# Filling only the empty rows of a row buffer with one scatter, and three loads and feature steps in another order

## The chip, the cores and the metric

The kernel runs on one core of a Trainium2 chip. The metric is the device time of one execution in microseconds (us), smaller is better. Three runs of the kernel before gave 189.14, 189.53 and 187.53 us, a median of 189.14. A core has five engines with a queue each: PE (matrix multiply, with its weight loads), DVE (vector), ACT (scalar), POOL (GpSimd) and SP (here it only issues transfers). Each engine works its own instructions in the order in which they were written; a semaphore makes one wait for another or for a transfer.

## The reference

```python
# q, k, v: (4, 4, 1088, 32) float32; S1, S2: (8, 32)
def phi(x):
    a = einsum('rd,bhsd->bhsr', S1, x); b = einsum('rd,bhsd->bhsr', S2, x)
    return einsum('bhsi,bhsj->bhsij', a, b).reshape(*x.shape[:-1], 64)
q_p, k_p = phi(q), phi(k)
kv = einsum('bhsf,bhsd->bhfd', k_p, v); z = sum(k_p, axis=2)
x  = einsum('bhsf,bhfd->bhsd', q_p, kv) / (einsum('bhsf,bhf->bhs', q_p, z)[..., None] + 1e-6)
x  = x.transpose(0, 2, 1, 3).reshape(4352, 128)          # rows: batch by position
expert = token_ids * 2654435761 % 8                      # 4352 ids
for e in range(8):                                       # w1[e]: 128x1024, w2[e]: 1024x128
    out[expert == e] = maximum(x[expert == e] @ w1[e], 0) @ w2[e]
```

## The kernel before

**Attention.** The four batches are worked one after the other in the order 0, 2, 1, 3 (counted b = 0 to 3 below). Each has 1024 "main" positions, held as 8 blocks of 128, and a "tail" of 64; the tails of two batches share one tile (`k_tail`, `v_tail`, `q_tail`). For a main tile of k or q, PE turns it (`kT_ps`, L460), ACT copies the turned blocks (`kT`, L465), PE multiplies by S1 and S2 (`abk_ps`, `abq_ps`, L486), ACT copies the first half (`first_of_ab`, L511) and DVE makes the 64 features (`kp` of k, `f` of q, L524, two instructions of 128x1024). PE then sums `kv` over positions (L557), turns the features of q (`fT_ps`, L575) and multiplies by `m`, the diagonal of `kv` (`x_ps`, L586). DVE normalizes in three chunks of three instructions (`den`, `den`, `xs`, L602 to L604). The tail of q goes the same way: `qTt_ps` (L471), `abqt_ps` (L501), `f_tail`, `fTt_ps` (L812). For b = 2 and 3, DVE's own 32x32 transposes turn q instead (`qT`, L494).

**Routing.** Every row goes to a slot of its expert. The ids (`tok`, `tok_tail`) give a mask, a scan and counts (`cnt`, L384), from which `place` (the expert's rank), `left` and the row number `sidx` come. An expert has 256 early slots and `cap` late ones, 313 for the first in rank and 5 fewer for each one behind it: 2048 + 2364 = 4412 slots for 4352 rows. Rows that fit no slot would be worked by a loop at the end (`turns`, L1128).

**The row buffer.** `x_rows` in device memory has a region of 256 + 4352 rows for each expert. Before any row is written, `fill_rows` fills the first 256 + 320 rows of each region with zeros and an id that no output row has (L207, four transfers), and 128 rows behind the regions (L210). POOL then scatters each normalized block of 128 rows into it by `sidx` (L609, 34 times), and SP fetches the rows expert by expert (`fetch`, L770).

**Experts.** Sixteen groups g (early and late slots of eight experts) are worked: PE `hp` (L912) and `op` (L920), ACT and DVE evict, rows come and go through SP and POOL. Between them DVE works `overflow_tables` in eight places.

**Order.** All five queues are written by hand. `pace` (L141) lets a large load start only when the third before it has landed. The loads stand on SP's queue in the order of the code; `tail(0)` of the ids and `tok` stand on ACT's queue, `tail(1)` on POOL's.

Of the kernel before, what the change touches and what calls it, by code (L numbers as in the profile page):

```python
# [30 lines left out]
def kernel(  # L31
# [35 lines left out]
    FL = -(-2 * GL // P) * P // 2  # L67
# [5 lines left out]
    OT = -(-(N - caps[-1]) // P)  # L73
# [51 lines left out]
    def load_tok():  # L125
# [69 lines left out]
    q_t.append(load_main(q, 1, "q"))  # L195
# [3 lines left out]

    def fill_rows():  # L200

        regions = x_dram[1:1 + E * XR].rearrange("(e m) d -> e m d", m=XR)
        h = P // 2
        for lo, hi, p in ((0, GE, P), (GE, GE + FL, h)):
            n = (hi - lo) // p
            for es in (slice(0, E // 2), slice(E // 2, E)):
                pace(nc.sync.dma_start(regions[es, lo:hi].rearrange("e (p n) d -> p e (n d)", n=n),  # L207
                                       empty_row[0:p, 0:n].rearrange("p n d -> p (n d)").unsqueeze(1)
                                       .to_broadcast([p, E // 2, n * XW])))
        nc.sync.dma_start(x_dram[1 + E * XR:], empty_row[:, 0])  # L210

# [180 lines left out]
    def route_places(cnt):  # L392
# [12 lines left out]
                                       op0=OP.mult, op1=OP.add)  # L405

# [425 lines left out]
    qTt = tail_turned(q_tail, "qTt_ps")  # L832
# [10 lines left out]
    for b in range(1, B):  # L843
# [156 lines left out]
    past = const.tile([P, OT, E], F32)  # L1000
    te = const.tile([P, OT], F32)
    begin = const.tile([P, OT], F32)

    def overflow_tables():
        nc.vector.scalar_tensor_tensor(nt[:], place[:], float(GD), left[:], op0=OP.mult, op1=OP.add)
        nc.vector.tensor_scalar(nt[:], nt[:], float(P - 1 - GL), 0.0, op0=OP.add, op1=OP.max)
# [19 lines left out]
        nc.vector.tensor_scalar(begin[:], begin[:], float(P), None, op0=OP.mult)
# [46 lines left out]
    for i in range(8):  # L1073
# [55 lines left out]
    with tc.If(turns > 0):  # L1129
        with tc.For_i(0, turns):  # L1130

            of = moe.tile([P, 2], F32, tag="of", name="of", bufs=1)
# [4 lines left out]
            nc.vector.tensor_scalar(turn[:], turn[:], 1.0, None, op0=OP.add)
            hot = moe.tile([P, E], F32, tag="hot", name="hot", bufs=1)
            picked = moe.tile([P, 2, E], F32, tag="picked", name="picked", bufs=1)
            own = moe.tile([P, 2], F32, tag="own", name="own", bufs=1)  # L1140
            V = nc.vector
            V.tensor_scalar(hot[:], iota[:, 0:E], of[:, 0:1], None, op0=OP.is_equal)
            for i, t in enumerate((place, left)):
                V.tensor_tensor(picked[:, i], hot[:], t[:], op=OP.mult)
# [78 lines left out]
```

## Time and profile before

| | us |
|---|---|
| runs | 187.53, 189.14, 189.53 (median 189.14) |
| profiled execution, its own time | 189.09 |
| its span | 187.4 |
| PE busy | 171.6 (92%) |
| DVE busy | 95.9 (51%) |
| POOL busy | 78.5 (42%) |
| ACT busy | 63.0 (34%) |
| moved by transfers | 28.54 MB |

The times that runs give are of whole executions; the span is from the first to the last thing that the profile sees in one of them, 1.7 us less. A stretch is given as start:end in us from the span's start. "PEclk" is the clock that PE was granted, as a share of full speed. A timeline row has its start, its length from the first to the last of its instructions, the engine, line, operation, what is written from what, and how many; in brackets how long the engine had been idle before it, and what ended that.

### The profile page before, as it was taken

The page shows a single profiled execution, that of the slowest core. Times are in us where ns is not written, and L with a number is a line of the kernel's source. Part 1 is how long each engine was busy: PE and PEld are TensorE (multiplying, and loading weights), DVE is VectorE, ACT ScalarE, POOL GpSimd, SP SyncE. Part 2 cuts the span into 40 slices and gives each one's busy share as a digit, 9 for nine tenths or more (in the row PEclk, how much of TensorE's full clock was granted, in tenths as well). Part 3 has the DMA queues.
Part 4 walks back from the last instruction along what each step waited for, and adds up shares of the span by engine and source line. Part 5 has one row for each costly group of instructions (what it writes and reads, how often), then busy time and mean ns, then how long its engine had stood idle before and what let it go on. Part 6 is the DMA issues. An engine that isn't in the chain of part 4 may idle for free. (4 is left out here: it accounts for less than half of the span.)

```text
span 187.4 us, 4151 instructions
## 1 busy us (share of the span) xinstructions
PE 171.6 (92%) x1526; PEld 142.2 (76%) x1526; DVE 95.9 (51%) x289; ACT 63.0 (34%) x160; POOL 78.5 (42%) x125
## 2 busy tenths in 40 slices
PE   7789809997979999999999999999999999999990
PEld 2569708997868888788888887777777777777990
DVE  3387634569895825346525535445254754524330
ACT  2277423552714323233233223232331313311320
POOL 7375047507787787144134122142240403335762
PEclk9999975999999999999999999999999999999998
DMA  3999999998517988966675694441323232130110
GB/s 97 307 265 282 204 271 344 354 323 263 161 61 166 306 174 196 215 174 169 108 189 143 116 173 91 96 99 38 88 58 89 70 84 69 28 84 29 45 36 28
DMA packets 45204, 28.54 MB, mean 152 GB/s; under 512 B 22065, under 2 KB 42546, under 8 KB 45183
## 3 DMA queue, kind: packets, MB, share of 16 engines
q1 hardware_dynamic: 41983, 23.57, 49.4%
q0 software_dynamic: 2240, 4.53, 8.5%
q8 instruction: 12, 0.20, 0.5%
q10 hardware_dynamic: 960, 0.17, 0.5%
q14 instruction: 9, 0.07, 0.1%
HBM read 17.42 MB, written 7.09 MB: 131 GB/s over the span
## 5 line engine op out<-in xcount | busy, mean ns | idle before, releaser
L920 PE MATMUL op<-hT,w 128*128 128x256 f32 (+8 forms) x256 | 76.4, 389 | 0.0
L923 POOL DMA_INDIRECT out_dram<-os,put x35 | 34.2, 977 | 74.6 <-DVE put L779 44.2
L709 DVE TENSOR_SCALAR hT<-hp 128x256 f32<-128x256 f32 (+9 forms) x68 | 29.1, 429 | 55.5 <-PE hp L912 46.3
L920 PEld LDWEIGHTS op<-hT,w 128*128 128x128 f32 x256 | 47.5, 190 | 10.5
L707 ACT ACTIVATE hT<-hp 128x256 f32<-128x256 f32 (+9 forms) x68 | 26.4, 390 | 65.0 <-PE hp L912 63.5
L912 PE MATMUL hp<-xT_late,w 128*128 128x313 f32 (+8 forms) x144 | 42.0, 386 | 0.2 <-DVE xT_late L805 0.2
L609 POOL DMA_INDIRECT x_rows<-xs,sidx x32 | 31.4, 982 | 24.4 <-DVE xs L604 8.6
L912 PE MATMUL hp<-xT,w 128*128 128x256 f32 x128 | 37.0, 380 | 0.3 <-issue 0.2
L912 PEld LDWEIGHTS hp<-xT_late,w 128*128 128x128 f32 x144 | 25.4, 190 | 7.2 <-issue 0.6
L912 PEld LDWEIGHTS hp<-xT,w 128*128 128x128 f32 x128 | 24.0, 190 | 4.0 <-issue 0.5
L524 DVE TENSOR_TENSOR f<-first_of_ab,abq_ps 128x1024 f32<-128x1024 f32 x8 | 9.4, 1214 | 5.8 <-ACT first_of_ab L511 5.8
L524 DVE TENSOR_TENSOR kp<-first_of_ab,abk_ps 128x1024 f32<-128x1024 f32 x7 | 8.3, 1217 | 5.6 <-ACT first_of_ab L511 5.4
L798 DVE COPY xh<-xg 128x256 uint16<-128x256 uint16 (+1 forms) x28 | 9.8, 391 | 0.0
L575 PE MATMUL fT_ps<-ident,f 128*128 128x128 f32 x64 | 8.2, 278 | 1.6 <-DVE f L524 1.6
L557 PE MATMUL kv<-va,kp 128*64 128x66 f32 x256 | 8.5, 222 | 1.0 <-issue 1.0
L576 ACT COPY fT<-fT_ps 128x512 f32<-128x512 f32 x16 | 8.3, 598 | 2.6 <-PE fT_ps L575 2.4
L557 PEld LDWEIGHTS kv<-va,kp 128*64 128x64 f32 x256 | 8.0, 138 | 1.3 <-issue 1.3
L575 PEld LDWEIGHTS fT_ps<-ident,f 128*128 128x128 f32 x64 | 6.9, 141 | 2.3 <-DVE f L524 2.0
L465 ACT COPY kT<-kT_ps 128x512 f32<-128x512 f32 x12 | 6.6, 588 | 5.4 <-PE kT_ps L460 5.4
L586 PE MATMUL x_ps<-m,fT 128*64 128x66 f32 x256 | 8.3, 223 | 0.0
L586 PEld LDWEIGHTS x_ps<-m,fT 128*64 128x64 f32 x256 | 7.8, 137 | 0.2 <-issue 0.2
L981 DVE COPY os<-turned 128x256 uint16<-128x256 uint16 (+1 forms) x26 | 7.2, 315 | 0.9 <-DMA turned<-half 0.7
(158 smaller groups left out, 137.1 us busy)
## 6 DMA issues: line engine op xcount, KB each, us to landing
w<-in_moe_w_dram SPq DMA_DIRECT2D x16, 512.0 KB
q<-in_q_dram SPq DMA_DIRECT2D x4, 512.0 KB
v<-in_v_dram SPq DMA_DIRECT2D x4, 512.0 KB
xg<-x_rows SPq DMA_DIRECT2D x12, 129.0 KB
k<-in_k_dram SPq DMA_DIRECT2D x3, 512.0 KB
x_rows<-empty_row SPq DMA_DIRECT2D x2, 660.0 KB
x_rows<-empty_row SPq DMA_DIRECT2D x2, 528.0 KB
out_dram<-os,put POOLq DMA_INDIRECT x35, 2.7
```

What stands on the lines that cost most here:

```text
L524: eng.tensor_tensor(dst, a[:, r].unsqueeze(3).to_broadcast(shape), ab[:, r].unsqueeze(2).to_broadcast(shape), op=OP.mult)
L557: nc.tensor.matmul(kv[HALVES[x], z], f[:, x], w.rearrange("p h d -> p (h d)"), start=(n == 0 and z == 0), stop=(n == T), skip_group_check= ...
L575: nc.tensor.transpose(p[:, j, z], f[:, (t0 + j) // Q, z, (t0 + j) % Q].rearrange("p h f -> p (h f)"), ident[:])
L576: nc.scalar.copy(fT[:, t0:t0 + 2], p[:])
L586: nc.tensor.matmul(p[x, j, z], fT[:, t0 + j, z, x], m[:, z], start=True, stop=True, skip_group_check=True)
L609: st_ = G_.indirect_dma_start(out=x_dram[:], out_offset=bass.IndirectOffsetOnAxis(ap=sidx[:, c:c + 1], axis=0), in_=row, in_offset=None, b ...
L707: nc.scalar.activation(dst, src, AF.Relu if relu else AF.Copy)
L709: return nc.vector.tensor_scalar(dst, src, 0.0, None, op0=OP.max).ins
L798: nc.vector.tensor_copy(xh[:, x * w:(x + 1) * w].rearrange("p (a b) -> p a b", a=n), xg3[k][:, 0:n].bitcast(U16).rearrange("p a (b two) -> ...
L912: last_mm[0] = nc.tensor.matmul(hp[:, 0:hi - lo], w1[:, g % E, c * P:(c + 1) * P], x_columns(first_of(g) + lo, first_of(g) + hi), start=Tr ...
L920: nc.tensor.matmul(ops[g][:, 0:hi - lo], w2[:, g % E, c], hTs[g][:, c, lo:hi], start=(c == 0), stop=(c == FC - 1))
L923: st_ = nc.gpsimd.indirect_dma_start(out=out[:], out_offset=bass.IndirectOffsetOnAxis(ap=idx, axis=0), in_=src, in_offset=None, bounds_che ...
```

## The change

The four fills of `x_rows` go. In their place DVE works out, while the counts are at hand, which rows of the slots are empty (`route_free`, seven instructions, and `route_free_end`, eight), and POOL scatters one block of 128 empty rows to them (`empty_rows`); indices without a row lie out of bounds and are dropped. With more than 128 empty slots the late rows would all go to the loop at the end, whose tables and body are written anew for that (`few`). `q`'s second main load stands behind the tails of k and v, and `q_tail` behind the third loads of k and q. Both tails of the ids are loaded by POOL. The steps of q's tail move into the loop of b = 1, and for the last q the features stand ahead of the normalization of b = 2.

On SP's queue, from the load of v of b = 0 (`v0`) to the tail of q; digits behind a name count batches, the last number is only a buffer's. Before:

```order
L159 DMA v0_107<-in_v_dram 128x4x256
L159 DMA q1_109<-in_q_dram 128x4x256
L151 DMA k_tail_111<-in_k_dram 64x8x32 x2
L151 DMA v_tail_114<-in_v_dram 64x8x32 x2
L207 DMA x_rows<-empty_row_154 128x4x264 x2
L207 DMA x_rows<-empty_row_154 64x4x660 x2
L210 DMA x_rows<-empty_row_154 128x132
L159 DMA v1_162<-in_v_dram 128x4x256
L151 DMA q_tail_164<-in_q_dram 64x8x32 x2
L159 DMA k2_167<-in_k_dram 128x4x256
L159 DMA q2_169<-in_q_dram 128x4x256
```

And of the change, the same stretch of SP's queue:

```order
L155 DMA v0_106<-in_v_dram 128x4x256
L147 DMA k_tail_108<-in_k_dram 64x8x32 x2
L147 DMA v_tail_111<-in_v_dram 64x8x32 x2
L155 DMA q1_155<-in_q_dram 128x4x256
L155 DMA v1_157<-in_v_dram 128x4x256
L246 DMA x_rows<-empty_row_152 128x132
L155 DMA k2_160<-in_k_dram 128x4x256
L155 DMA q2_162<-in_q_dram 128x4x256
L147 DMA q_tail_164<-in_q_dram 64x8x32 x2
```

The four fills between the tails and `v1` are gone, `q1` stands behind the tails, and `q_tail` behind `q2`.

On PE's queue, from the turning of the second q to the sums of b = 1. Before:

```order
L460 MATMUL kT_ps_522<-ident_117,q1_109 128x128 x4
L471 MATMUL qTt_ps_569<-ident_117,q_tail_164 128x128 x2
L486 MATMUL abq_ps_574<-s_k_215,kT_520 64x4x16 x8
L486 MATMUL abq_ps_574<-s_k_215,kT_527 64x4x16 x8
L460 MATMUL kT_ps_593<-ident_117,k2_167 128x128 x4
L460 MATMUL kT_ps_600<-ident_117,k2_167 128x128 x4
L501 MATMUL abqt_ps_607<-s_k_215,kT_tail_572 64x64 x4
L557 MATMUL kv_620<-va1_145,kp_530 64x66 x32
```

And of the change:

```order
L484 MATMUL kT_ps_543<-ident_114,q1_155 128x128 x4
L510 MATMUL abq_ps_590<-s_k_211,kT_541 64x4x16 x8
L510 MATMUL abq_ps_590<-s_k_211,kT_548 64x4x16 x8
L484 MATMUL kT_ps_609<-ident_114,k2_160 128x128 x4
L484 MATMUL kT_ps_616<-ident_114,k2_160 128x128 x4
L581 MATMUL kv_628<-va1_143,kp_551 64x66 x32
L581 MATMUL kv_628<-va_tail1_141,kp_tail_230 64x66 x4
L495 MATMUL qTt_ps_670<-ident_114,q_tail_164 128x128 x2
L599 MATMUL fT_ps_676<-ident_114,f_623 128x128 x4
```

The turning of q's tail (`qTt_ps`) moved from ahead of `abq_ps` to behind the sums of b = 1; its products follow the four `fT_ps`.

On DVE's queue, at b = 2: the features of the last k (`kp`), the normalization of b = 2 (`den`, `xs2`) and the features of the last q (`f`). Before:

```order
L524 TENSOR_TENSOR kp_991<-first_of_ab_953,abk_ps_932 128x1024 x2
L602 TENSOR_SCALAR den_1013<-x_ps_956 128x12
L603 RECIPROCAL den_1013<-den_1013 128x12
L604 TENSOR_TENSOR xs2_191<-x_ps_956,den_1013 128x3x128
L602 TENSOR_SCALAR den_1026<-x_ps_969 128x12
L603 RECIPROCAL den_1026<-den_1026 128x12
L604 TENSOR_TENSOR xs2_191<-x_ps_969,den_1026 128x3x128
L602 TENSOR_SCALAR den_1039<-x_ps_982 128x8
L603 RECIPROCAL den_1039<-den_1039 128x8
L604 TENSOR_TENSOR xs2_191<-x_ps_982,den_1039 128x2x128
L524 TENSOR_TENSOR f_1049<-first_of_ab_1011,abq_ps_994 128x1024 x2
```

And of the change:

```order
L548 TENSOR_TENSOR kp_1012<-first_of_ab_974,abk_ps_953 128x1024 x2
L548 TENSOR_TENSOR f_1034<-first_of_ab_1032,abq_ps_1015 128x1024 x2
L626 TENSOR_SCALAR den_1037<-x_ps_977 128x12
L627 RECIPROCAL den_1037<-den_1037 128x12
L628 TENSOR_TENSOR xs2_187<-x_ps_977,den_1037 128x3x128
```

The two feature instructions `f` moved ahead of the nine of the normalization. The diff, without the loop at the end:

```diff
         def tail(x, eng):
             eng.dma_start(tok_tail[half_rows(x)], ids[2 * x:2 * x + 2, SM:].rearrange("u s two -> s u two"))
-        tail(0, nc.scalar)
         nc.scalar.dma_start(tok[:].rearrange("p (b t) two -> p b (t two)", b=B),
                             ids[:, 0:SM].rearrange("b (p t) two -> p b (t two)", t=T))
-        return lambda: tail(1, nc.gpsimd)
+        return lambda: [tail(x, nc.gpsimd) for x in range(TT)]
...
-    q_t.append(load_main(q, 1, "q"))
     k_tail = load_tail(k, "k_tail")
     v_tail = load_tail(v, "v_tail")
-    def fill_rows():
-        regions = x_dram[1:1 + E * XR].rearrange("(e m) d -> e m d", m=XR)
...
-    empty_row = const.tile([P, 2 * FL // P, XW], F32)
+    empty_row = const.tile([P, XW], F32)
...
-    fill_rows()
+    q_t.append(load_main(q, 1, "q"))
     v_t.append(load_main(v, 1, "v"))
-    q_tail = load_tail(q, "q_tail")
+    nc.sync.dma_start(x_dram[1 + E * XR:], empty_row[:])
     k_t.append(load_main(k, 2, "k"))
     q_t.append(load_main(q, 2, "q"))
+    q_tail = load_tail(q, "q_tail")
...
+    def route_free(cnt):
+        V = nc.vector
+        V.tensor_tensor(free[:, 0], took[:], cnt[:, 1, 0], op=OP.subtract)
+        V.scalar_tensor_tensor(free[:, 1], place[:], -float(GD), left[:], op0=OP.mult, op1=OP.subtract)
+        V.tensor_scalar(free[:, 1], free[:, 1], float(GL), 0.0, op0=OP.add, op1=OP.max)
+        V.tensor_tensor_scan(free_to[:].rearrange("p k e -> p (k e)"), ones[:, 0:NC * E],
+                             free[:].rearrange("p k e -> p (k e)"), 0.0, op0=OP.mult, op1=OP.add)
+        V.tensor_copy(row_at[:, 0], cnt[:, 1, 0])
+        V.tensor_scalar(row_at[:, 1], left[:], float(GE), None, op0=OP.add)
+        V.scalar_tensor_tensor(row_at[:], place[:].unsqueeze(1).to_broadcast([P, NC, E]), float(XR), row_at[:],
+                               op0=OP.mult, op1=OP.add)
+    def route_free_end():
...
+        V.tensor_scalar(eidx[:], row[:], float(FAR), None, op0=OP.add)
+    def empty_rows():
+        st_ = G_.indirect_dma_start(
+            out=x_dram[:], out_offset=bass.IndirectOffsetOnAxis(ap=eidx[:], axis=0),
+            in_=empty_row[:], in_offset=None, bounds_check=E * XR, oob_is_err=False)
...
     abt = tail_products(kTt, "abt_ps")
+    route_free(cnt)
     tail_features(kp_tail, first_copied(abt))
     route_early()
+    route_free_end()
+    empty_rows()
...
-    qTt = tail_turned(q_tail, "qTt_ps")
     abq = side_ab(qT, "abq_ps")
     firsts = first_copied(flat(abq))
     kT = side_turned(k_t[2])
-    abt = tail_products(qTt, "abqt_ps")
     f = all_features(firsts, "f", 1)
-    tail_features(f_tail, first_copied(abt))
...
         if b == 1:
             qT = q_blocks(q_t[2])
+            qTt = tail_turned(q_tail, "qTt_ps")
...
         fT = f_all(f)
         if b == 1:
-            tail_f_turned(f_tail)
+            tail_features(f_tail, first_copied(tail_products(qTt, "abqt_ps")))
...
         x_ps = x_all(b)
+        if b == 1:
+            tail_f_turned(f_tail)
...
+        if b == 2:
+            f = all_features(firsts, "f", 1)
         x_normalized(b, x_ps)
         if b == 1:
             x_tail(0, fT_tail)
             scatter_tail(0)
-        if more:
             f = all_features(firsts, "f", 1)
-        if b == 1:
             qT = q_blocks(q_t[3])
...
-    for i in range(8):
+    for i in range(5):
         at(G - 5 + i // 4, 2 * (i % 4), next, tables, None)
...
     with tc.If(turns > 0):
+        nc.gpsimd.drain()
         with tc.For_i(0, turns):
```

More of the change, by code (lines that the diff above doesn't have):

```diff
@@ L72 @@
     GAP = (ST - HT) * P - sum(caps)
-    OT = -(-(N - caps[-1]) // P)
+    OT = -(-(E * GE + N) // P) + E
     WARM = 9
@@ L405, in route_places @@
                                        op0=OP.mult, op1=OP.add)
+    free = const.tile([P, NC, E], F32)
+    free_to = const.tile([P, NC, E], F32)
+    row_at = const.tile([P, NC, E], F32)
+    nth = const.tile([P, NC, E], F32)
+    eidx = const.tile([P, 1], I32)
+    def route_free(cnt):
[10 more added lines that the diff above has]
+    def route_free_end():
+        V = nc.vector
+        within = const.tile([P, NC, E], F32, name="within")
+        V.tensor_tensor(nth[:], free[:], free_to[:], op=OP.subtract)
+        V.tensor_scalar(nth[:], nth[:], p1[:], None, op0=OP.add)
+        V.tensor_tensor(within[:], nth[:], free[:], op=OP.is_le)
+        V.scalar_tensor_tensor(within[:], nth[:], 0.0, within[:], op0=OP.is_gt, op1=OP.mult)
+        V.tensor_tensor(row_at[:], row_at[:], nth[:], op=OP.add)
+        V.scalar_tensor_tensor(row_at[:], row_at[:], -float(FAR), within[:], op0=OP.add, op1=OP.mult)
+        row = const.tile([P, 1], F32, name="row_of_free")
+        V.tensor_reduce(row[:], row_at[:].rearrange("p k e -> p (k e)"), axis=AX.X, op=OP.add)
+        V.tensor_scalar(eidx[:], row[:], float(FAR), None, op0=OP.add)
[3 more added lines that the diff above has]
+            in_=empty_row[:], in_offset=None, bounds_check=E * XR, oob_is_err=False)
+        tc.declare_no_dep(st_.ins, group="x_rows", reason="distinct rows")
+        tc.add_to_no_dep_group("x_rows", st_.ins)
     def route_rows(u, dst):
@@ L999 @@
     n_over = const.tile([P, 1], I32)
-    past = const.tile([P, OT, E], F32)
-    te = const.tile([P, OT], F32)
-    begin = const.tile([P, OT], F32)
+    begin = const.tile([P, E], F32)
+    few = const.tile([P, 1], F32)
     def overflow_tables():
-        nc.vector.scalar_tensor_tensor(nt[:], place[:], float(GD), left[:], op0=OP.mult, op1=OP.add)
-        nc.vector.tensor_scalar(nt[:], nt[:], float(P - 1 - GL), 0.0, op0=OP.add, op1=OP.max)
+        nc.vector.tensor_scalar(few[:], free_to[:, 1, E - 1:E], float(P), None, op0=OP.is_le)
+        nc.vector.tensor_scalar(begin[:], place[:], -float(GD), float(GL + GE), op0=OP.mult, op1=OP.add)
+        yield
+        nc.vector.tensor_tensor(begin[:], begin[:], few[:].to_broadcast([P, E]), op=OP.mult)
+        nc.vector.tensor_tensor(nt[:], left[:], begin[:], op=OP.subtract)
+        yield
+        nc.vector.tensor_scalar(nt[:], nt[:], float(GE + P - 1), 0.0, op0=OP.add, op1=OP.max)
         nc.vector.tensor_copy(nt_i[:], nt[:])
@@ L1138 @@
-            hot = moe.tile([P, E], F32, tag="hot", name="hot", bufs=1)
[L1139 to L1144, printed above, removed]
+            V = nc.vector
+            late_of = moe.tile([P, E], F32, tag="late_of", name="late_of", bufs=1)
@@ new lines @@
+            of = moe.tile([P, 1], F32, tag="of", name="of", bufs=1)
+            hot = moe.tile([P, E], F32, tag="hot", name="hot", bufs=1)
+            picked = moe.tile([P, 5, E], F32, tag="picked", name="picked", bufs=1)
+            own = moe.tile([P, 5], F32, tag="own", name="own", bufs=1)
+            V.tensor_tensor(late_of[:], ends[:], turn[:].to_broadcast([P, E]), op=OP.is_le)
+            V.tensor_reduce(of[:], late_of[:], axis=AX.X, op=OP.add)
+            V.tensor_scalar(hot[:], iota[:, 0:E], of[:], None, op0=OP.is_equal)
@@ L1145 @@
+            V.tensor_tensor(picked[:, 0], ends[:], nt[:], op=OP.subtract)
+            V.tensor_tensor(picked[:, 0], picked[:, 0], hot[:], op=OP.mult)
+            for i, t in enumerate((begin[:], place[:], left[:], cnt[:, 1, 0])):
+                V.tensor_tensor(picked[:, 1 + i], hot[:], t, op=OP.mult)
             V.tensor_reduce(own[:], picked[:], axis=AX.X, op=OP.add)
-            at = moe.tile([P, 4], F32, tag="at", name="at", bufs=1)
+            at = moe.tile([P, 6], F32, tag="at", name="at", bufs=1)
@@ new lines @@
+            V.tensor_scalar(at[:, 2:3], at[:, 0:1], float(GE), None, op0=OP.is_gt)
+            V.tensor_tensor(at[:, 1:2], at[:, 1:2], at[:, 2:3], op=OP.max)
+            V.tensor_scalar(at[:, 3:4], own[:, 3:4], float(GE), None, op0=OP.add)
+            V.tensor_tensor(at[:, 3:4], at[:, 0:1], at[:, 3:4], op=OP.is_le)
+            V.tensor_tensor(at[:, 1:2], at[:, 1:2], at[:, 3:4], op=OP.mult)
+            V.scalar_tensor_tensor(at[:, 4:5], own[:, 2:3], float(XR), at[:, 0:1], op0=OP.mult, op1=OP.add)
```

55 lines of the change are left out of this document (14 added, 41 removed).

## The prediction

> **What bounds the kernel now.** I read the page first, for the engine that is busiest:
>
> ```profile
> PE 171.6 (92%) x1526; PEld 142.2 (76%) x1526; DVE 95.9 (51%) x289; ACT 63.0 (34%) x160; POOL 78.5 (42%) x125
> ```
>
> PE leaves 187.4 - 171.6 = 15.8 us of the span. The second view was busy time by stretch (columns: length, then busy us of PE, PEld, DVE, ACT and POOL with instruction counts, granted clock, share of the transfer engines, GB/s):
>
> ```profile
> 21.50:27.85 6.35, 1.07 (x11) 0.86 (x9) 3.43 (x9) 1.88 (x3) 1.85 (x2) 0.85 0.97 242
> 27.85:32.73 4.88, 4.88 (x51) 4.10 (x52) 1.86 (x2) 1.95 (x5) 3.66 (x5) 0.50 1.05 345
> 38.93:57.50 18.57, 15.74 (x394) 14.44 (x390) 17.41 (x38) 7.29 (x16) 11.66 (x12) 1.00 0.59 184
> 61.55:183.00 121.45, 121.06 (x553) 99.51 (x553) 56.64 (x195) 34.87 (x99) 44.16 (x46) 1.00 0.49 113
> ```
>
> The experts (61.55 on) are PE without a gap, so what is gained there has to be gained by starting them earlier. The hole is 21.50 to 27.85, with the transfer engines full, and behind it PE works 4.88 us at half its clock. From 38.93 to 57.50 DVE is the full engine (17.41 of 18.57) and PE has slack. The third view, PE's waits (total, times, longest), names what ends the holes:
>
> ```profile
> PE qTt_ps L471 <- DMA q_tail<-in_q_dram: 5.3, 1, 5.3
> PE fT_ps L575 <- DVE f L524: 1.6, 1, 1.6
> PE cnt L384 <- ACT cp L379: 1.3, 1, 1.3
> PE kv L557 <- issue: 1.0, 1, 1.0
> ```
>
> All four lie in the attention, and the change touches the first three. The 1.0 us of "issue" waits for nothing that the profile shows.
>
> **Part 1: the fills and q's tail.** PE's timeline around the hole; the first two rows are the same work at full clock elsewhere:
>
> ```profile
> 12.69 1.09 PE L460 MATMUL kT_ps<-ident,k 128*128 128x128 f32 x8
> 40.14 1.10 PE L486 MATMUL abq_ps<-s_k,qT 128*64 128x64 f32 x32
> 21.48 1.09 PE L460 MATMUL kT_ps<-ident,q 128*128 128x128 f32 x8
> 27.85 0.66 PE L471 MATMUL qTt_ps<-ident,q_tail 128*128 128x128 f32 x2 [5.28 <-DMA q_tail<-in_q_dram]
> 28.44 1.98 PE L486 MATMUL abq_ps<-s_k,kT 128*64 128x64 f32 x32
> 30.34 1.97 PE L460 MATMUL kT_ps<-ident,k 128*128 128x128 f32 x8
> 32.24 0.67 PE L501 MATMUL abqt_ps<-s_k,kT_tail 128*64 128x64 f32 x8
> 32.73 2.06 PE L557 MATMUL kv<-va,kp 128*64 128x66 f32 x64
> ```
>
> `qTt_ps` waits for its load, and all of PE's queue stands behind it. Its load was late because of what stands ahead of it on SP's queue (the page's sizes, then SP's timeline):
>
> ```profile
> x_rows<-empty_row SPq DMA_DIRECT2D x2, 660.0 KB
> x_rows<-empty_row SPq DMA_DIRECT2D x2, 528.0 KB
> ```
>
> ```profile
> 8.57 0.37 SPq L159 DMA_DIRECT2D q<-in_q_dram  x1
> 11.87 6.29 SPq L207 DMA_DIRECT2D x_rows<-empty_row  x4
> ```
>
> The fills are 2 x 660 + 2 x 528 = 2376 KB, and `v1` stands behind them too. In the change the fills are gone. What is late next? ACT's and DVE's rows say it:
>
> ```profile
> 22.17 1.07 ACT L465 COPY kT<-kT_ps 128x512 f32<-128x512 f32 x2 [2.08 <-PE kT_ps L460]
> 27.04 1.05 ACT L541 COPY va<-v 128x1024 f32<-128x1024 f32 x1 [3.80 <-DMA v<-in_v_dram]
> ```
>
> ```profile
> 16.70 0.69 DVE L524 TENSOR_TENSOR kp_tail<-first_of_ab,abt_ps 128x512 f32<-128x512 f32 x1 [0.83 <-ACT first_of_ab L511]
> 20.12 1.22 DVE L524 TENSOR_TENSOR kp<-first_of_ab,abk_ps 128x1024 f32<-128x1024 f32 x1 [1.75 <-ACT first_of_ab L511]
> 23.12 1.21 DVE L524 TENSOR_TENSOR kp<-first_of_ab,abk_ps 128x1024 f32<-128x1024 f32 x1
> 38.93 2.35 DVE L524 TENSOR_TENSOR kp<-first_of_ab,abk_ps 128x1024 f32<-128x1024 f32 x2 [3.66 <-ACT first_of_ab L511]
> ```
>
> `va` of b = 1 needs `v1`, which landed at 27.04. Even at 345 GB/s, the best stretch above, the fills took 2376 x 1.024 / 345 = 7.1 us of the transfer engines, so `v1` lands by 20.0, ahead of 23.24, where ACT is done with `kT` and turns to it. `k2` (512 KB) stands right behind, 2.2 us more at 242 GB/s, so about 22.2, wanted at 23.8. `q1` now stands behind four tail loads, but it had waited for `q0` until 8.57 anyway, and it is wanted only at 21.48.
>
> So, from 21.48: both `kT` copied at 23.24, the second half of `abq_ps` behind it to 23.8, `k2` turned (1.09) to 24.9. `kv` there needs `va` (23.24 + 1.05 = 24.3) and the second `kp` (24.33, and later by part 2). I take 24.9 against 32.73: 7.8 earlier. Of this the wait is 5.28; the half clock is (1.98 - 1.10) + (1.97 - 1.09) and half of 0.66 + 0.67, 2.4; the two tail steps left this place (0.7 at full clock), and a wait for ACT's copies of about 0.6 shows that the hole had covered.
>
> The two tail steps come back behind `kv` (half of 0.66 and 0.67), while the turning of `f_tail` leaves the way to DVE's `kp` at 38.93 (row below, 0.60). `kv` to `kp` was 38.93 - 32.73 = 6.2, and becomes 6.2 + 0.7 - 0.6 = 6.3: `kp` at 31.2 instead of 38.93, 7.7 earlier. From there on DVE is the full engine, so this is what carries on.
>
> ```profile
> 36.75 0.60 PE L812 MATMUL fTt_ps<-ident,f_tail 128*128 128x128 f32 x4
> ```
>
> That turning (0.60) now stands between `kp` and PE's next `kv`, in the stretch that DVE fills: PE's slack there is 18.57 - 15.74 = 2.8, of which 1.6 lies at `fT_ps`, 1.0 is the "issue" hole, and 0.2 is left. If the hole stays, 0.6 - 0.2 = 0.4 reaches DVE; if it goes, nothing. I take 0.4 off.
>
> *On the clock.* The granted clock was 0.50 all the way from 27.85 to 32.73, though PE was busy throughout, so the recovery took above 4 us and is priced above at 2.4. The Trainium skill ("TensorE: Matmul & The Clock Gate", Part 1) says that an idle window of about 3.4 us halves PE's clock and a busy one of about 3.4 us restores it, so by it the pause would cost 3.4 x 0.5 = 1.7, and the sum would gain 0.7 less. The trace shows the halving; its recovery is longer here, and the row decides.
>
> **Part 2: what DVE and POOL get.** Fifteen small DVE instructions of 128x8 or 128x16. The nearest rows are six of `route_places`, from here to the `f` behind them:
>
> ```profile
> 12.38 0.17 DVE L394 SCALAR_TENSOR_TENSOR left<-took,counts 128x8 f32<-128x8 f32 x1
> 13.53 2.34 DVE L524 TENSOR_TENSOR f<-first_of_ab,abq_ps 128x1024 f32<-128x1024 f32 x2
> ```
>
> (13.53 - 12.38) / 6 = 0.19 each; my bounds are 0.17, the row's own length, and 0.28, half as much again. Seven are 1.3 us where DVE idled 0.83: `kp_tail` ends 0.5 later, at 17.9. Eight more are 1.5, with 0.5 carried over, where DVE idled 1.75: `kp` at 20.12 comes 0.3 later, the second at 24.6 instead of 24.33, still ahead of PE's 24.9. So 0; at 0.28 the fifteen take 1.3 more, 24.6 becomes 25.9, and 1.0 is lost. A gain is excluded, since nothing leaves DVE there.
>
> POOL gets one scatter more, and its scatters of rows no longer wait for the fills (the page's group: busy, mean ns, then idle time ahead and its longest releaser):
>
> ```profile
> L609 POOL DMA_INDIRECT x_rows<-xs,sidx x32 | 31.4, 982 | 24.4 <-DVE xs L604 8.6
> ```
>
> The 8.6 stands ahead of the first scatter; the `xs` it names follows the `kp` of 20.12 by a microsecond or so, so it was the fills that ended late. Without it the eight scatters of b = 0 start at about 22.5 and stand at most (31.4 + 24.4 - 8.6) / 32 = 1.5 apart, so they are through by 34.5. The first rows of b = 1 come about 0.9 behind `kp` at 31.2 + 2.35, at 34.5 too. The empty rows' scatter (0.98) stands ahead, at about 20.6, before any row is there: 0. The smaller fill of `empty_row` and eight overflow steps that become five run in DVE and POOL time that nobody waits for: 0.
>
> **Part 3: the ids.** `tail(0)` leaves ACT's queue, so `tok` is issued earlier; POOL works a second such load.
>
> ```profile
> 1.90 0.74 ACTq L130 DMA_DIRECT2D tok_tail<-in_moe_token_ids_dram  x1
> 7.75 0.18 DVE L367 TENSOR_SCALAR eid_i<-tok 128x32 int32<-128x32 int32 x1 [2.20 <-DMA tok<-in_moe_token_ids_dram]
> 10.37 1.95 POOL L524 TENSOR_TENSOR kp<-both_of_ab 128x1024 f32<-128x1024 f32 x1 [3.80 <-ACT counts L387]
> ```
>
> DVE waits 2.20 for `tok`, and PE's `cnt` stands 1.3 behind that chain. ACT issues `tok` 0.74 earlier, but it then shares the transfer engines with the first k. I take 0.6, between 0 (k delayed as much) and 1.3 (all of `cnt`'s wait). POOL's second load, about as long as ACT's, is covered by its 3.80 of idle time.
>
> **Part 4: features ahead of the normalization.** At b = 2:
>
> ```profile
> 50.24 2.35 DVE L524 TENSOR_TENSOR kp<-first_of_ab,abk_ps 128x1024 f32<-128x1024 f32 x2
> 52.81 0.37 ACT L511 COPY first_of_ab<-abq_ps 128x256 f32<-128x256 f32 x1 [2.23 <-issue]
> 55.14 2.34 DVE L524 TENSOR_TENSOR f<-first_of_ab,abq_ps 128x1024 f32<-128x1024 f32 x2
> 59.54 0.17 DVE L602 TENSOR_SCALAR den<-x_ps 128x12 f32<-128x12 f32 x1 [2.05 <-PE x_ps L586]
> 60.67 0.41 PE L789 MATMUL xp<-ident,xg 128*128 128x128 f32 x2
> ```
>
> On before's time axis: `f` can start when ACT has copied, 53.2, not 55.14, and PE's wait of 1.58 goes. The normalization (55.14 - 52.59 = 2.55) then runs 55.5 to 58.1, and the next one behind it without the 2.05 of idle time. The first transposed rows `xp` need the memory bank of its first chunk, at 58.1 + about 1.0 = 59.1 instead of 60.67. That caps the gain at 1.4; I take 1.3 (0.5 if the fetched rows come in late, which were not waited for at 60.67).
>
> **The sum.** 7.7 - 0.4 + 0 + 0.6 + 1.3 = 9.2 us, all ahead of the experts, whose 121 us of PE only move; 0.1 goes to a second branch on every engine at the end. 189.09 - 9.1 = 180.0 us. The profiled execution stands at the median of the runs (189.14), so I forecast 180.0 for the median too. The unknowns put together, 0.6 + 1.0 + 0.8 against the forecast and 0.7 + 0.4 for it, give 178.9 to 182.4 for this case.
>
> **The rivals.**
>
> *Another load takes over.* `v1` or `k2` is late. For: the transfer engines were full (0.97 to 1.05) up to here. Against: 7.1 us of their work went. If `v1` came only at 27.04 as before, `kv` starts at 28.1: 3.2 lost, 183.2, and up to 2.2 more if the clock falls again, 185.4.
>
> *DVE becomes the bound.* The fifteen instructions at 0.28, 1.0, and 0.3 more where the stretch from 38.93 is DVE's already: 181.3.
>
> *Part 4 gives nothing*, because the fetch of the first rows (on POOL's scatters of b = 1) decides: 181.3.
>
> *Slower: the scatter of empty rows stalls POOL.* 4412 - 4352 = 60 slots are empty if every row finds a slot, so 68 of 128 indices are dropped. If a dropped index were dear, POOL's chain slips, and with it the fetch of the first rows and the experts. The scatter starts 1.9 us ahead of the first rows (20.6 to 22.5), so it would have to take 1.9 + 9.1 = 11 us for the whole gain to go, 10 / 68 = 0.15 per dropped row; at twice that the time is 190 + 10 = 200. Against it:
>
> ```profile
> L923 POOL DMA_INDIRECT out_dram<-os,put x35 | 34.2, 977 | 74.6 <-DVE put L779 44.2
> ```
>
> These 35 scatters drop the same empty rows, and their mean is 0.977, against 0.982 for the rows that are all written.
>
> *The loop at the end is entered.* It is if a row finds no slot or more than 128 are empty. Before's execution ends without it, so every row has a slot and 60 are empty. I give it nothing of its own.
>
> **How the numbers follow.** Forecast 0.74 (178.9 to 182.4), another load 0.07 (183.2 to 185.4), DVE 0.08 and part 4 0.06 (181.3 each), slower 0.04, no change 0.01. The likeliest is 180.0. For 8 in 10 the range takes the forecast's bounds, widened a little for what the runs scatter, and the near end of the late load: 178.3 to 183.8. The runs of before lie 1% apart, so under 1% (187.2 to 191.0) counts as no change. Faster is 0.74 + 0.07 + 0.08 + 0.06 = 0.95, same 0.01, slower 0.04.
>
> **What would show it.** Right: no PE wait for `q_tail`; PE's clock at 1.00 from 10 us on; `kv` of b = 1 at about 24.3 and DVE's third `kp` pair at about 30.6; `cnt`'s wait near 0.7; `fT_ps` of the last b without a wait for `f`; the first `hp` at about 52.5 instead of 61.55; 2.4 MB less moved. Wrong: a wait of PE or ACT above 1 us for `v`, `k` or `q`; a clock of 0.50 anywhere; a POOL scatter above 2 us; `xp` waiting for `xg`.

## The result, and the profile after

The kernel after the change took 179.43 us (median of 4 runs, 179.25 to 180.8), beside 189.09 us before on the same chip: a ratio of 0.952, 95% interval 0.945 to 0.959. The prediction on record was 180.0. The profiled execution took 179.45 us, with a span of 177.7 instead of 187.4, 9.7 less.

That holds for this chip. On a second one the change itself was not timed, but three variants of it were, with ratios of 0.951 to 0.955. On two further chips the kernel before itself took 218 us. The change was timed on one of these and was slower there: 222.21 us, ratio 1.018 (1.014 to 1.022). What differs there is shown below; the prediction said nothing of it.

The page after, its first line:

```profile
PE 169.8 (96%) x1525; PEld 140.3 (79%) x1526; DVE 96.4 (54%) x300; ACT 63.0 (35%) x160; POOL 79.7 (45%) x127
```

PE's busy time fell by 1.8 us, though no matmul was taken away. It fell in the attention (50.5 to 48.6 us up to the first `hp`; the experts took 121.1 and 121.2), where the stretch at half clock is gone. The transfers moved 26.14 MB instead of 28.54, the 2.4 less that were predicted. PE leaves 177.7 - 169.8 = 7.9 us of the span instead of 15.8. Busy time by stretch after, with the columns as before (length, then PE, PEld, DVE, ACT, POOL, granted clock, share of the transfer engines, GB/s), over the places of the four rows shown of before:

```profile
20.24:23.69 3.45, 3.21 (x52) 2.74 (x48) 3.25 (x9) 2.72 (x5) 2.09 (x3) 1.00 1.03 323
23.69:28.00 4.31, 4.31 (x91) 4.14 (x90) 3.81 (x6) 2.62 (x8) 3.12 (x4) 1.00 0.88 293
29.95:48.00 18.05, 17.63 (x416) 16.14 (x414) 16.35 (x35) 9.10 (x20) 10.10 (x12) 1.00 0.64 207
51.14:172.60 121.46, 120.36 (x548) 98.64 (x549) 54.93 (x191) 34.91 (x98) 46.79 (x50) 1.00 0.52 117
```

The hole is gone (0.24 us idle of 3.45), and the clock is 1.00 where it was 0.50. The transfer engines are as full as they were (1.03), but now with loads that somebody waits for. In the third stretch PE has 0.4 us of slack left, where it had 2.8. In the fourth, the experts, PE lost 0.7 more than before (121.46 - 120.36 = 1.1, instead of 0.4). PE's waits after (total, times, longest), without the first one for a constant:

```profile
PE hp L939 <- ACT half L987: 0.8, 1, 0.8
PE kT_ps L484 <- DMA k<-in_k_dram: 0.3, 1, 0.3
...
PE fT_ps L599 <- DVE kp_tail L548: 0.2, 1, 0.2
PE xp L816 <- DVE den L626: 0.2, 1, 0.2
```

The waits of 5.3, 1.6 and 1.3 us that headed this list before are not in it; nor is the 1.0 us of "issue". A new one heads it, 0.8 us in the experts. The profile names ACT's `half` for it, but DVE's `xT`, the transposed rows that `hp` works on, ends in the same instant (69.70). In the kernel before `hp` starts at 79.48, 0.1 us behind `xT`, while `half` still runs (79.34 to 79.99), so it is `xT` that PE waits for. PE's timeline through the changed places:

```profile
8.43 0.17 PE L368 MATMUL cnt<-cp,before 128*128 128x16 bf16 x1
...
20.24 1.09 PE L484 MATMUL kT_ps<-ident,q 128*128 128x128 f32 x8
21.57 1.17 PE L510 MATMUL abq_ps<-s_k,kT 128*64 128x64 f32 x32 [0.24 <-ACT kT L489]
22.67 1.09 PE L484 MATMUL kT_ps<-ident,k 128*128 128x128 f32 x8
23.69 2.10 PE L581 MATMUL kv<-va,kp 128*64 128x66 f32 x64
...
25.95 0.44 PE L495 MATMUL qTt_ps<-ident,q_tail 128*128 128x128 f32 x2
...
45.79 1.97 PE L599 MATMUL fT_ps<-ident,f 128*128 128x128 f32 x16
...
50.26 0.41 PE L816 MATMUL xp<-ident,xg 128*128 128x128 f32 x2 [0.20 <-DVE den L626]
...
51.14 1.99 PE L939 MATMUL hp<-xT,w 128*128 128x256 f32 x8
...
69.80 0.67 PE L939 MATMUL hp<-xT,w 128*128 128x256 f32 x2 [0.81 <-ACT half L987]
```

Read as leads over before: `cnt` 1.47 us (9.90 to 8.43), the turning of the second q 1.24 (21.48 to 20.24), `kv` of b = 1 9.04 (32.73 to 23.69), `xp` 10.41 (60.67 to 50.26), the first `hp` 10.41 (61.55 to 51.14). Of these 10.41, 9.7 reach the end. DVE's feature pairs give the steps between (the third and the last `kp`, the last `f`):

```profile
29.95 2.35 DVE L548 TENSOR_TENSOR kp<-first_of_ab,abk_ps 128x1024 f32<-128x1024 f32 x2
...
41.28 2.35 DVE L548 TENSOR_TENSOR kp<-first_of_ab,abk_ps 128x1024 f32<-128x1024 f32 x2
44.24 2.35 DVE L548 TENSOR_TENSOR f<-first_of_ab,abq_ps 128x1024 f32<-128x1024 f32 x2 [0.62 <-ACT first_of_ab L535]
```

The lead is 8.98 at the third pair and 8.96 at the last (before: 38.93 and 50.24), so what was won ahead of 30 us went through the stretch undiminished; the last `f` follows its `kp` by 0.6 us of waiting for ACT, and no longer by a normalization.

### The profile page after: what moved, and what is told of

Its sections match the earlier page's. It is cut to its first block, busy times and chain, and to the rows that moved or that the text cites. A ratio compares the mean times of both kernels' runs of the same rounds, so it can differ in the third digit from the quotient of the medians.

```text
span 177.7 us, 4160 instructions
## 1 busy us (share of the span) xinstructions
PE 169.8 (96%) x1525; PEld 140.3 (79%) x1526; DVE 96.4 (54%) x300; ACT 63.0 (35%) x160; POOL 79.7 (45%) x127
## 2 busy tenths in 40 slices
DMA packets 43524, 26.14 MB, mean 147 GB/s; under 512 B 21913, under 2 KB 41370, under 8 KB 43503
## 5 line engine op out<-in xcount | busy, mean ns | idle before, releaser
L736 DVE TENSOR_SCALAR hT<-hp 128x256 f32<-128x256 f32 (+9 forms) x68 | 29.1, 428 | 57.4 <-PE hp L939 47.1
L987 ACT COPY half<-op 128x256 uint16<-128x256 uint16 x16 | 5.2, 375 | 7.4 <-PE op L947 7.4
```

Source lines behind the costliest of these rows:

```text
L736: return nc.vector.tensor_scalar(dst, src, 0.0, None, op0=OP.max).ins
```

## The experiments

Ratios are to the kernel before on the same chip. The first four ran on one chip, where before took 188.85 us.

**The fills put back.**

```diff
...
     q_t.append(load_main(q, 1, "q"))
+    regions = x_dram[1:1 + E * XR].rearrange("(e m) d -> e m d", m=XR)
+    for lo, hi, p in ((0, GE, P), (GE, GE + FL, P // 2)):
...
+            pace(nc.sync.dma_start(regions[es, lo:hi]..., fill_row[0:p, 0:n]...))
     v_t.append(load_main(v, 1, "v"))
```

> The kernel after the change, with the four fills of x_rows put back on SP between the loads of q1 and v1; q's tail stays late, and everything else stays changed. Theory (the fills made the wait, and what stands first behind them gets it): v1 lands at 25 to 27 us again, as before, so va of b = 1 and with it kv come 2.5 to 4.5 us behind 23.69, PE waits for a load or for va, and if that wait passes 3.4 us the clock falls to 0.50 and 1 to 2 us more are lost: 183 to 186 us, with a PE gap of 3 to 5 us between 21 and 28 us. Rival (the place of q's tail made the wait, the fills were covered): no gap above 1 us, 179.4 to 180.0 us.

Measured: 187.45 us (10 runs), ratio 0.993 (0.990 to 0.996). PE in its profile, and its granted clock from the end of the wait on:

```profile
22.60 1.17 PE L521 MATMUL abq_ps<-s_k,kT 128*64 128x64 f32 x32 [0.24 <-ACT kT L500]
28.86 1.94 PE L495 MATMUL kT_ps<-ident,k 128*128 128x128 f32 x8 [5.09 <-DMA k<-in_k_dram]
30.73 3.67 PE L592 MATMUL kv<-va,kp 128*64 128x66 f32 x64
```

```profile
28.86:30.73 1.87, 1.87 (x9) 1.54 (x9) 1.55 (x3) 0.58 (x1) 1.26 (x3) 0.50 1.18 214
30.73:32.50 1.77, 1.77 (x33) 1.77 (x34) 1.30 (x2) 0.58 (x1) 1.47 (x2) 0.50 1.09 339
...
33.50:34.23 0.73, 0.73 (x20) 0.73 (x18) 0.00 (x0) 0.00 (x0) 0.59 (x1) 0.56 1.04 363
34.23:36.00 1.77, 1.77 (x27) 1.70 (x24) 0.00 (x0) 1.26 (x4) 1.30 (x2) 1.00 0.99 295
```

The wait came back at nearly its old length, 5.09 us instead of 5.28, but for another load: `k2` stands behind the fills and `v1` now. So it was the fills, and PE waits for the load behind them that it needs first. With them back, 0.041 of the 0.048 is lost, 7.8 us of 189 (6.8 to 7.4 beside the three other variants on this chip): that is what taking the fills away is worth on top of the rest. The time is 1.45 us beyond the expectation's upper end: PE waited for `k2`, not for `v1`, and the half clock cost 2.4 us, since it lasted through `kT_ps` and nearly all of `kv` (28.86 to 34.23, 5.37 us, for what takes 2.95 after the change, 22.67 to 25.62).

**Only the tail of q put back.**

```diff
     nc.sync.dma_start(x_dram[1 + E * XR:], empty_row[:])
+    q_tail = load_tail(q, "q_tail")
...
+    qTt = tail_turned(q_tail, "qTt_ps")
     abq = side_ab(qT, "abq_ps")
...
+    abt = tail_products(qTt, "abqt_ps")
     f = all_features(firsts, "f", 1)
+    tail_features(f_tail, first_copied(abt))
...
```

> The kernel after the change, without fills, but with q's tail loaded right behind v1 and turned and multiplied where it was before (between q1's turning and kv of b = 1). Theory (the fills alone made the wait): q's tail lands by 21 us and PE does not wait for it; two tail steps of 0.35 us each stand ahead of kv again, so kv and the third kp pair come 0 to 0.6 us later: 179.4 to 180.0 us, clock 1.00. Rival (the tail had to be moved as well, because the transfer engines are full there anyway): PE waits 1 us or more for q_tail, 180.8 us or more.

Measured: 180.1 us (6 runs), ratio 0.951 (0.945 to 0.956), no different from the change itself. PE does not wait for `q_tail`:

```profile
22.03 0.38 PE L495 MATMUL qTt_ps<-ident,q_tail 128*128 128x128 f32 x2
```

From the turning of the second q, `kv` of b = 1 comes 3.90 us later (21.10 to 25.00) instead of 3.45, and the last `kv` 23.70 instead of 23.34. Moving the tail is worth 0.4 us in the profile and nothing that the times can show; the rival is out. Two waits appear here that the change's own profile does not have. One is a pause of 0.68 us ("issue") in the `kv` of b = 2 (35.95), where the kernel before has one of 0.99 (44.01). The other is 0.65 us of `xp` waiting for the fetched rows `xg` (51.93), the limit that the prediction had named for part 4.

**The ids' tail on ACT again.**

```diff
+        tail(0, nc.scalar)
         nc.scalar.dma_start(tok[:].rearrange("p (b t) two -> p b (t two)", b=B),
...
-        return lambda: [tail(x, nc.gpsimd) for x in range(TT)]
+        return lambda: tail(1, nc.gpsimd)
```

> The kernel after the change with the first half of the ids' tail loaded on ACT's queue ahead of tok again, as before. Theory (the whole chain tok, counts, cnt is on the path, and the change gained 1.24 us there, not the 0.6 that was predicted): cnt comes about 1.3 us later, and all behind it 1.2: 180.6 us. As predicted (0.6 us): 180.0 us. Rival (something else of the change moved cnt, or the hole of the 21 us mark takes it up): 179.4 us.

Measured: 180.22 us (7 runs), ratio 0.953 (0.949 to 0.957). The intervals of this ratio and of the change's overlap, so the times don't tell 0.6 from 1.2 us. The execution that was profiled took 182.64 us, longer than the others, mostly in the experts; only its start is read here. It shows the old wait:

```profile
10.35 0.17 PE L369 MATMUL cnt<-cp,before 128*128 128x16 bf16 x1 [1.28 <-ACT cp L364]
```

`cnt` starts 2.43 us behind `abk_ps` (7.92) instead of 1.21 (7.22 to 8.43), 1.2 later: the order of the ids makes this wait. How much of it lasts is not shown. The turning of the second q stands 13.93 us behind `abk_ps` here and 13.02 after the change, but it stands 13.59, 13.87 and 14.45 behind it in the three other profiles of this chip, which have the change's ids and a `cnt` at 1.09 to 1.57. In these PE waits 0.35 to 0.47 us for `kp_tail`, and here it does not, so part of what an early `cnt` gains goes to that wait. That the chain is on the path with more than the 0.6 predicted is thus the reading of one profile.

**The last q's features behind the normalization again.**

```diff
-        if b == 2:
-            f = all_features(firsts, "f", 1)
         x_normalized(b, x_ps)
+        if b == 2:
+            f = all_features(firsts, "f", 1)
```

> The kernel after the change with the last q's features behind the normalization of b = 2 again, as before. Theory: PE waits about 1.6 us for f at fT_ps again and the experts start 1.4 us later (hp at 52.5 instead of 51.14), but the transposing loads of the experts then have their old lead, and the new wait of 0.8 us ahead of group 3 of the experts goes: 180.0 us in all. Rival (that wait does not hang on where the experts start): 180.8 us. Rival (the fetch decides the experts' start, not f): 179.4 us.

Measured: 180.62 us (6 runs), ratio 0.955 (0.951 to 0.960).

```profile
48.81 2.22 PE L599 MATMUL fT_ps<-ident,f 128*128 128x128 f32 x16 [1.57 <-DVE f L548]
```

The wait is there as before (1.58), and the first `hp` follows the last `kv` by 8.98 us (44.96 to 53.94) instead of 7.56 (43.58 to 51.14): 1.42. PE has no wait for `half` in the experts of this run. The time lies between the two theories (180.0 and 180.8) and doesn't choose. The missing wait speaks for the first, but the run with the fills back goes against it. There the fetch leads `hp` by 3.5 us (56.24 to 59.73), as after the change (47.80 to 51.14, 3.3), with expert 3's weights issued as close to `hp` (1.4 and 1.2 ahead), and yet PE doesn't wait. DVE's joining of transposed rows shows what differs. After the change, then with the fills back:

```profile
61.13 0.62 DVE L832 COPY xT<-xh_turned 128x256 uint16<-128x256 uint16 x2 [2.56 <-DMA xh_turned<-xh]
68.98 0.72 DVE L832 COPY xT<-xh_turned 128x256 uint16<-128x256 uint16 x2 [1.68 <-DMA xh_turned<-xh]
```

```profile
68.64 0.61 DVE L843 COPY xT<-xh_turned 128x256 uint16<-128x256 uint16 x2 [1.49 <-DMA xh_turned<-xh]
76.22 0.73 DVE L843 COPY xT<-xh_turned 128x256 uint16<-128x256 uint16 x2 [0.42 <-DMA xh_turned<-xh]
```

The first transposing load took 5.7 us from its issue to this row after the change (55.47 to 61.13), 4.6 with the fills back (64.04) and 4.3 in this run (58.14 to 62.40), for the same issue time behind `hp` (4.33, 4.31, 4.20). The second row stands 17.8 us behind the first `hp` after the change, and 16.5 to 17.3 behind it where PE has no such wait (before, and with the fills, the tail or the features put back). So the 0.8 us goes with how long the first transposing load takes; that it is the cause was not tested, and why the load's time differs is open.

The next eight runs fell on two other chips, on which the kernel before took 218.06 and 218.15 us. What they were to tell of the whole time is covered by something else there; what they tell of single places follows.

**The change itself on such a chip.**

> The kernel after the change itself, unchanged, beside the three others on the same chip. If this chip supplies PE's instructions without pauses, as in the first profile after: 179.4 us, 0.952 of before. If PE's stretches of kv show pauses for which nothing in the profile is the cause, of 0.3 to 1.1 us each, as in the runs where the kernel before took 218 us: above 215 us and no gain on before.

Measured: 222.21 us (6 runs), ratio 1.018 (1.014 to 1.022): slower. PE's waits, longest first:

```profile
PE hp L939 <- ACT xT L734: 12.7, 1, 12.7
PE kv L581 <- issue: 12.3, 19, 1.1
```

The 12.3 us are 19 pauses in the middle of `kv`, work of one kind that waits for no engine and no load. Three of them, and the last row scatter of POOL's string beside them:

```profile
27.62 0.39 PE L581 MATMUL kv<-va,kp 128*64 128x66 f32 x5 [1.08 <-issue]
29.05 0.52 PE L581 MATMUL kv<-va,kp 128*64 128x66 f32 x4 [1.04 <-issue]
...
33.32 1.84 PE L581 MATMUL kv<-va,kp 128*64 128x66 f32 x29 [1.14 <-issue]
```

```profile
31.00 0.98 POOL L633 DMA_INDIRECT x_rows<-xs,sidx  x1 [0.31 <-issue]
```

The pauses go from 25.1 to 33.3 us and POOL's scatters from 21.98 to 31.98; the next from 47.1 to 57.5, the scatters from 44.71 to 55.96. The third string has fourteen scatters without a break, from 70.63 to 88.30, and in it ACT and DVE stand as well, for nothing that the profile names ("remote"), until both go on together behind it:

```profile
90.48 0.17 DVE L626 TENSOR_SCALAR den<-x_ps 128x8 f32<-128x8 f32 x1 [9.56 <-remote]
90.52 0.38 ACT L734 ACTIVATE xT<-xp 128x256 f32<-128x256 f32 x1 [19.11 <-remote]
90.96 3.78 PE L939 MATMUL hp<-xT,w 128*128 128x256 f32 x8 [12.72 <-ACT xT L734]
```

On the first chip the same scatters run at the same pace (1.28 us each) beside a PE that doesn't pause after the change. Single pauses of the kind occur on the first two chips too: the 0.99 us of the kernel before and the 0.68 with the tail back each begin 0.5 us behind the start of POOL's second string (42.49 and 34.75). The transfer engines are not what is short, in the second string they are 0.14 busy:

```profile
44.71:58.00 13.29, 6.47 (x86) 4.76 (x84) 6.50 (x17) 1.07 (x2) 8.81 (x9) 0.79 0.14 47
```

So on these chips three engines pause in and just behind POOL's strings of scatters. That they are short of instructions then is what a pause without a cause suggests. The larger loads of instructions in the trace don't show it: they are 12 of 16 KB on both chips, each 0.9 to 1.4 us long here and 0.9 to 1.6 after the change on the first, and only one falls among the eight pauses from 25.1 to 33.3. No run took the scatters away, so that they are the cause is not shown either, and why these chips differ is open.

**PE kept busy through the wait, in the kernel before.**

```diff
+    keep_busy(20)
     qTt = tail_turned(q_tail, "qTt_ps")
```

> The kernel before the change, with 20 matmuls on constant data (512 columns each, results never read) put ahead of the turning of q's tail, so that PE is busy through most of its 5.28 us wait; the wait for the load itself stays. Theory by the rows of the profile (the half clock behind the wait costs 2.4 us): clock 1.00 from 27.85 on, kv of b = 1 at 30.3 instead of 32.73, 186.7 us. By a recovery of 3.4 us (1.7 us lost): 187.4 us. Rival (the half clock is covered by ACT, DVE or transfers there): 189.1 us.

> The kernel before with 20 matmuls on constant data (512 columns each, results never read) in PE's 5.28 us wait for q's tail, once more, since the first time PE's pauses covered the effect. By the rows (half clock costs 2.4 us): clock 1.00 from the wait on, 2.4 us less than before, ratio 0.987. By a recovery of 3.4 us: 1.7 us less, 0.991. Rival (the half clock is covered by other engines): ratio 1.000.

Measured: ratios 1.014 (1.007 to 1.021) and 1.015 (1.009 to 1.020), on the chips with the pauses. That is slower than before, which no theory had, and why is open, so none of them can be read from the time. The place itself lies ahead of the first pause (31.38). The second run:

```profile
22.63 4.54 PE L256 MATMUL idle<-warm 128*128 128x512 bf16 x20
28.07 0.41 PE L471 MATMUL qTt_ps<-ident,q_tail 128*128 128x128 f32 x2 [0.91 <-DMA q_tail<-in_q_dram]
28.41 1.15 PE L486 MATMUL abq_ps<-s_k,kT 128*64 128x64 f32 x32
29.50 1.09 PE L460 MATMUL kT_ps<-ident,k 128*128 128x128 f32 x8
30.52 0.45 PE L501 MATMUL abqt_ps<-s_k,kT_tail 128*64 128x64 f32 x8
30.80 0.34 PE L557 MATMUL kv<-va,kp 128*64 128x66 f32 x5
```

From `qTt_ps` to `kv` it takes 2.73 us (2.82 in the first run) at a clock of 1.00, where before took 4.88 at 0.50 on the first chip. The half clock cost 2.1 us there: the 2.4 predicted was 0.3 too much, the 1.7 that follows from a recovery of 3.4 us 0.4 too little.

**The fifteen DVE instructions twice.**

```diff
...
     route_free(cnt)
+    route_free(cnt)
     tail_features(kp_tail, first_copied(abt))
...
+    route_free_end("a")
     route_free_end()
```

> The kernel after the change with the fifteen DVE instructions that find the empty slots done twice (the second result unused where it must not count). Theory (DVE has no idle time left from 14.6 to 26 us in the profile after, and the second kp ends only 0.5 us ahead of kv): 2.7 us more of DVE, 2.2 us more at kv and at the end, 181.6 us; the fifteen themselves lay on the edge of the path. Rival (covered, as the prediction had it at 0): 179.4 to 179.8 us.

> The kernel after with the fifteen DVE instructions that find the empty slots done twice, once more. Theory (DVE is full from 14.6 to 26 us): 2.2 us above the kernel after of the same call, with a wait of PE for kp_tail of 1 to 1.5 us ahead of fT's last quarter and kv of b = 1 as much later. As predicted (covered): within 0.5 us of it.

Measured: 222.0 and 221.95 us, the second with a ratio of 1.017 (1.013 to 1.021) beside 1.018 for the change itself. Up to the first pauses, the second run:

```profile
17.71 0.46 PE L582 MATMUL kv<-va_tail,kp_tail 128*64 128x66 f32 x8 [0.88 <-DVE kp_tail L549]
...
24.36 1.16 PE L582 MATMUL kv<-va,kp 128*64 128x66 f32 x32
25.82 0.74 PE L582 MATMUL kv<-va,kp 128*64 128x66 f32 x17 [0.29 <-issue]
```

From the start of `fT_ps` (14.85) `kv` of b = 1 comes 9.51 us later, instead of 9.13 in the change itself on that chip (15.18 to 24.31), and its second half 0.29 later again, right behind the second `kp` (24.55 + 1.21). So 0.7 us for 2.7 us more of DVE. The theory of 2.2 is out: it took `kv` to need both `kp` at its start, but it needs the second only for its second half, about 1.1 us on. The instructions are nearly covered.

**The fourth expert's weights ahead of the fetch; seven DVE instructions behind `kp_tail`.** The first run has the first part of the edit alone, the two others both.

```diff
-    route_free(cnt)
     tail_features(kp_tail, first_copied(abt))
+    route_free(cnt)
...
-            for ld in lds[:6]:
+            for ld in lds:
                 pace(ld())
             for k in range(4):
                 fetch(k)
-            for ld in lds[6:]:
-                pace(ld())
```

> The kernel after the change with the weights of the fourth expert loaded ahead of the fetch of the first rows on SP, in the stretch from 36 to 48 us where SP and the transfer engines have little to do. Theory (the new wait of 0.8 us ahead of the experts' third group comes of the transposing loads sharing the transfer engines with weights that now lie 2 us later relative to PE): the wait goes, 178.6 us. Rival (the transposing loads are late because the fetch or the rows are, not through the weights): the wait stays, 179.4 us. Rival (SP issues the fetch later for it): above 179.4 us.

> As the run before it, and the first seven of the DVE instructions that find the empty slots stand behind kp_tail's features instead of ahead of them, so that the memory bank of the tail's products is free 1.1 us earlier. Theory: the wait of 0.22 us of fT_ps for kp_tail goes, 0.2 us less than the run before it, 178.4 us. Rival (DVE is the chain there, so the order does not matter): the same as the run before it, 178.6 us.

> The kernel after with the fourth expert's weights loaded ahead of the fetch of the first rows and seven of the DVE instructions behind kp_tail's features, once more. Theory: PE's wait for kp_tail (0.2 to 0.5 us) and its wait ahead of the experts' third group (0.8 us) both go: 0.6 to 1.2 us less than the kernel after of the same call. Rival (the transposing loads are late for another reason): the wait ahead of the third group stays and the gain is 0.2 to 0.5 us.

Measured: 222.55 us, 1.016 (1.009 to 1.023); 221.0, 1.014 (1.008 to 1.020); 221.06, 1.015 (1.010 to 1.019). The experts' waits can't be compared on these chips, so the first part says nothing and stays open. The second part shows in the profile: the wait of `fT_ps` for `kp_tail` (0.36 in the change itself on such a chip) is gone in the two runs with both parts, and from the start of `fT_ps` to the turning of the second q it takes 5.13 us instead of 5.67. ACT takes most of that back (0.59 instead of 0.24 of waiting for `kT`): `kv` comes 8.94 and 8.96 behind `fT_ps` instead of 9.13, 0.2 us earlier.

## Why the prediction was right, point by point

**The bound, and part 1: right.** The hole came from the fills, and the queue behind them was what PE waited for. The lead at `kv` of b = 1 is 9.04 us, of which 1.24 stood already at the turning of the second q; the 7.8 that remain are the number predicted. From `kv` to the third `kp` pair it takes 6.26 us (predicted 6.3). Putting the fills back costs 7.8 us. Two sizes inside it were off and cancelled: the half clock cost 2.1 and not 2.4, and the wait for ACT's copies that the hole had covered was 0.24 and not 0.6.

On the clock, the trace records when it fell and rose. It stood at 0.50 from 25.92 to 32.75 us before and from 27.31 to 34.14 with the fills back, 6.83 us both times, and PE worked through the last 4.9 and 5.3 of them. Apart from the one at the end of each execution, every stretch at half clock in these traces lasted a whole multiple of 3.41 us (3.41 to 20.48). The rule that the prediction weighed (the Trainium skill, "TensorE: Matmul & The Clock Gate", Part 1: at least one busy window of about 3.4 us restores the clock, and the windows run freely, not from the first matmul) agrees with that. What does not hold is the price of 1.7 that was taken from it, which counts a single window from the first matmul: the window in which PE began to work, idle for its first 1.9 and 1.6 us, did not count, so two passed at half clock.

**The 0.4 taken off for the "issue" hole: wrong.** The hole was not there, the middle of the attention ran without it (8.98 of lead at the third pair, 8.96 at the last), and nothing was lost. That the change removes it is not shown, since the run with the tail put back has 0.68 us of it in the same `kv`.

**Part 2, DVE and POOL: right as to the scatter, a little off as to DVE.** POOL's scatters after:

```profile
19.22 1.12 POOL L425 DMA_INDIRECT x_rows<-empty_row,eidx  x1 [3.45 <-DVE eidx L422]
21.37 1.01 POOL L633 DMA_INDIRECT x_rows<-xs,sidx  x1 [1.03 <-DVE den L626]
```

The scatter of empty rows took 1.12 us with its 68 dropped indices, so the rival that ends slower fell by its own number, 11 us. The fifteen instructions were put at 0; they cost 0.22 us at `fT_ps`, and 0.2 us at `kv` come back where seven of them make way.

**Part 3, the ids: right in mechanism, too small in this profile.** `cnt`'s wait of 1.34 went whole, and 1.24 reached the turning of the second q. The step that failed is "it then shares the transfer engines with the first k. I take 0.6": PE waited for `k` only 0.3, and `tok` came much earlier than its issue. ACT issued it 0.8 us earlier (1.88 instead of 2.67), and DVE worked on it 2.3 us earlier, at 5.46 instead of 7.75, without a wait:

```profile
5.46 0.17 DVE L351 TENSOR_SCALAR eid_i<-tok 128x32 int32<-128x32 int32 x1
```

Profiles with the same order of ids differ by over a microsecond at the second q, so the 1.24 is not a safe size.

**Part 4: right.** 1.43 by the change (10.41 at `hp` less 8.98), 1.42 by taking it back, 1.3 predicted; and the cap was the one named, `xp` waiting 0.20 for the normalization. (The prediction's rows give that cap as 60.67 - 59.1 = 1.6, not the 1.4 that it states.)

**The step that failed in the sum** is "all ahead of the experts, whose 121 us of PE only move". The attention gave 10.41 us and not 9.2, mostly through the ids (0.6 more) and the 0.4; the experts then lost 0.7, with a wait of 0.81 behind late transposed rows. The two partly cancel: 180.0 was 0.6 off, for a sum whose terms were off by more. That it came so close is in part luck.

**What it did not see** is that the gain was measured only on chips on which PE does not pause in this way. Its rivals were all of this kernel's waits, and the only one that ends slower was the wrong one. On the chips with pauses the change leads by 3.3 us at `slots_ps` of the last batch (63.18 beside 66.51 in the kernel before with PE kept busy) and then loses it: its first `hp` stands at 90.96, the other's here:

```profile
85.48 1.99 PE L913 MATMUL hp<-xT,w 128*128 128x256 f32 x8
```

In the other the third string of scatters has eight and ends at 80.97, and the next starts beside the experts. That part 4 makes the string long, because it puts the two last normalizations one behind the other, follows from the code, but no run tested it there.

## What to carry to other kernels

Bulk writes that nobody waits for are not free on a queue that also issues loads: look at what stands first behind them, and count the half clock that a pause of PE leaves behind. Sum a change at several marks along the path, not only at the end, since terms that are off can cancel. And where a string of indirect transfers runs beside fine-grained matmuls, time the change on more than one chip before calling it a gain.

## What the runs showed of the hardware

On two chips the kernel before took 218 us instead of 189. In the profiles taken there, of the change and of near variants, PE, ACT and DVE paused while POOL worked strings of indirect scatters, with the transfer engines 0.14 busy in one of them. In the profile of the change there and the second one with PE kept busy, the pauses set in 1.3 to 5.4 us behind a string's start, and were over between 0.7 us ahead of its end and 2.2 behind it.

PE's clock fell to 0.50 in waits of 5.1 and 5.3 us, 3.5 and 3.4 us behind their start, and rose 6.83 us later both times, so that 5.3 and 4.9 us of continuous work ran at half clock. Where PE was kept busy through the wait, it stayed at 1.00 there. All stretches at half clock ahead of an execution's end lasted whole multiples of 3.41 us.

A transposing load of the same rows took between 4.3 and 5.7 us from its issue until DVE worked on what it brought, at the same distance from the work around it. A scatter of 128 indices of which 68 are dropped took 1.12 us of POOL, beside 0.98 for 128 rows that are all written.
